# Second products of the first four chunks of a fused attention and softplus network: from one product of 512 columns to two of 256, all but the last of each block

## The chip, the cores and the metric

The kernel runs on one core of a Trainium2 chip. The metric is device time in microseconds (us) for one execution, and a kernel's time is the median of its runs. TensorE (PE in the profile) makes the matrix products; each product has a weight load of its own (PEld), which brings the stationary operand. VectorE (DVE) and ScalarE (ACT) do element work, and SyncE (SP) issues the transfers.

## The reference, cut to what matters

```
k_p, v_p = mean over 8 rows of k, v           # 576 rows become 72
attn     = softmax(q k_p^T / 8)               # 8 batches, 8 heads, head size 64
x        = attn v_p, as 4608 tokens x 512
h        = x @ w_in                           # 512 -> 2048      "first products"
g        = max(h, 0) + log1p(exp(-|h|))       # softplus
out      = g @ w_out                          # 2048 -> 512      "second products"
```

All is float32. A product of float32 accuracy is made of three products in a rounded float32 form (float32r): each operand is split into a high and a low part, and high x high, high x low and low x high are added in PSUM.

## The kernel before

The 4608 tokens are cut in 18 chunks of 256 (two tiles of 128 tokens). The 2048 hidden features are 16 groups of 128. For one chunk and one group, the first products make `h` (128 features x 256 tokens): four blocks of 128 input features, three products each, so 12 products with 256 moving columns (the tokens, `x`), the weights being stationary. ACT makes softplus of it twice, once rounded (`gh`) and once in full, and DVE subtracts to get the low part `gl`. The second products have 128 tokens of `gh` or `gl` as the stationary operand, and the weights `wo` (512 output columns) move. They add up in `acc`, one PSUM bank of 128 x 512 for each token tile.

There are three regimes:

- Chunks 0 to 2 (`feed`) run while the weights are still being loaded and split into high and low parts. First products are line 514, second products line 536 (`ffn2`): for each group 2 token tiles x 3 products, so 6 products of 512 columns, and 48 such blocks.
- Chunk 3 takes two groups at once (`pair1`, line 562, and `pair2`, line 603): 2 tiles x 2 groups x 3 = 12 products of 512 columns in each of 8 blocks.
- Chunks 4 to 17 save products with sums of quarters (`pair2_fast`, line 710). Here all products, first and second, have 256 columns. The second products take quarters of `wo` (its columns 0 to 255 or 256 to 511) or combined sums as the moving operand. The change doesn't touch them.

The order of the work is made while the program is built: a planner (`Order.run`) lists operations with estimated costs, in us, and places them engine by engine; each engine then runs its own list in that order and waits by semaphores. The second products are one operation each there, with written costs:

```
before2 = op(PE, 1.4, second, ...)          # feed: one ffn2 block
o = p2[c, u] = op(PE, 2.8, fn, wait, ...)   # chunk 3: one pair2 block
```

The `x` of chunks 0, 1, 3 and all later ones lies in two pairs of buffers of `xpool`; that of chunk 2 lies in the slots `Sa`, `Sb`, which later hold sums (`new_x`). In the built program's placement a partition's first byte of `wo`'s moving rows is at 64 modulo 128, in both halves of 256 columns, and all stationary `gh` and `gl` are at 0 modulo 128. For the first products the weights (stationary) are at 0 modulo 128, and `x` (moving) at 64 for all chunks but chunk 2, whose `x` is at 0.

Of the kernel before, what the change touches and what calls it, by code (L numbers as in the profile page):

```python
# [103 lines left out]
def pooled_attention_softplus_ffn(  # L104
# [9 lines left out]
    nc = tc.nc  # L114
    nc.scalar.preload_act_table_set("exp_and_others")
    B, H, S, D = q.shape
    NTOK, DM = out.shape
# [6 lines left out]
    T = 2  # L124
# [3 lines left out]
    FC = DFF // P  # L128
# [4 lines left out]
    FP = FC // 2  # L133
    O2 = DM // 2
# [367 lines left out]
    gs, accs = {}, {}  # L502
# [19 lines left out]
    def split_g(c, f, name):  # L522
# [2 lines left out]
        nc.vector.tensor_tensor(out=gl, in0=g, in1=gh.bitcast(F32), op=ALU.subtract)  # L525
        gs[c, f] = gh, gl

    def ffn2(c, f):
        if f == 0:
            accs[c] = [psum.tile([P, DM], F32, tag=b, name="acc") for b in acc_banks]  # L530
        gh, gl = gs.pop((c, f))
        hi, lo = wo[f]
        for t in range(T):
            ts = slice(t * P, (t + 1) * P)
            for j, (a, w) in enumerate(((gh, hi), (gh, lo), (gl, hi))):
                nc.tensor.matmul(out=accs[c][t], lhsT=a[:, ts], rhs=w,  # L536
                                 start=f == 0 and j == 0, stop=f == FC - 1 and j == 2)

    def copy_out(c, t, tag):
        o = one.tile([P, DM], F32, tag=tag, name="o")  # L540
# [53 lines left out]
    def pair2(c, u):  # L594

        if u == 0:
            accs[c] = [psum.tile([P, DM], F32, tag=b, name="acc") for b in acc_banks]
        g, gh, gl = gs.pop((c, u))
        for t in range(T):
            for k in range(2):  # L600
                hi, lo = wo[2 * u + k]
                for j, (a, w) in enumerate(((gh, hi), (gh, lo), (gl, hi))):
                    nc.tensor.matmul(out=accs[c][t], lhsT=a[:, 2 * k + t], rhs=w,  # L603
                                     start=u == 0 and k == 0 and j == 0,
                                     stop=u == FP - 1 and k == 1 and j == 2)

# [449 lines left out]
    def feed(c):  # L1058
        before1 = before2 = None
        acc_slots[c] = [Slot("bank") for _ in range(T)]  # L1060
        for f in range(FC):
            s, n, g, gh, gl = (Slot(x) for x in ("bank", "h", "g", "gh", "gl"))
            before1 = op(PE, 1.4, lambda f=f, s=s: ffn1_products(c, f, bank(s, "h")),
                         [before1, *x_done[c], *converted[f]], [s, n, *(acc_slots[c] if f == 0 else [])],
                         rest=8.4 * (FC - f) - LATER * c, first=LEAD * (N1 - 1 - c))
            a = op(ACT, act(CT), lambda f=f, s=s, gh=gh: softplus(c, f, s.tile, "gh" + gh.name), [before1, *exps],
                   [s, gh], table="softplus")
            d = op(ACT, act(CT), lambda f=f, s=s, g=g: softplus(
                c, f, s.tile, g.name), [a], [s, n, g], table="softplus")
            d = op(DVE, dve2(CT), lambda f=f, s=gl: split_g(c, f, s.name), [a, d], [g, gh, gl])  # L1070

            def second(f=f):
                if f == 0:
                    acc_banks[:] = [s.name for s in acc_slots[c]]
                ffn2(c, f)
            if (c, f) != (N1 - 1, FC - 1):
                before2 = op(PE, 1.4, second, [before2, d], [gh, gl, *acc_slots[c]],
                             rest=8.4 * (FC - f) - LATER * c + 6, first=200)
# [239 lines left out]
    def second_products(c, u, before):  # L1318
        fast = c >= NF
        wait, slots = p2[c, u]  # L1320
        wait = [before, *wait, *(t_ready.get(u, ()) if fast else ())]
        if u == 0:
            banks_of[c] = [Slot("acc") for _ in range(4 if fast else T)]
        banks = banks_of[c]

        def fn(which=(1, 2, 6, 7, 5, 3, 4)):
            if u == 0:
                (m_banks if fast else acc_banks)[:] = [s.name for s in banks if s.name]
            if fast:
                if u == 0 and which[0] == 5:  # L1330
                    m_banks[:] = m_banks[2:]
                pair2_fast(c, u, which)
            else:
                pair2(c, u)
        if not fast:
            o = p2[c, u] = op(PE, 2.8, fn, wait, [*slots, *banks])
            if u == FP - 1:
                output(c, [o], banks)
        elif u in (0, FP - 1):
            i, o = drained.get(c - 1, (None, None)) if u == 0 else (None, None)  # L1340
            i = op(PE, 12 * MM, lambda: fn((1, 2, 6, 7)), [*wait, i], [*slots, *banks[:2]])
            o = p2[c, u] = op(PE, 9 * MM, lambda: fn((5, 3, 4)), [i, o], [*slots, *banks[2:]])
            if u == FP - 1:
                output(c, [i, o], banks)
        else:
            o = p2[c, u] = op(PE, 21 * MM, fn, wait, [*slots, *banks])
        return o
# [25 lines left out]
    def last_of_first(before):  # L1373
        s = taken
        o = op(PE, 1.4, lambda: ffn2(N1 - 1, FC - 1), [before], s[:4])
        output(N1 - 1, [o], s[:T])
        return o
# [61 lines left out]
```

## Time and profile before

| | |
|---|---|
| median of 3 runs | 898.61 us (898.35 to 899.19) |
| the profiled execution's own time | 899.0 us |
| its span, first to last instruction | 897.3 us |
| granted TensorE clock | 0.998 |
| PE busy | 884.1 us, 99% of the span, 8308 products |
| DVE busy | 649.5 us, 72% |
| ACT busy | 407.7 us, 45% |
| line 536 (512 columns) | 288 products, 46.4 us to 190.5 us |
| line 603 (512 columns) | 96 products, 194.2 us to 243.5 us |

A busy PE says little, since products overlap and their ends are modelled: a product of 256 columns is given some 279 ns and the next starts long before. What a product costs is the distance from its start to the next one's start, and that is what the prediction reads from the timeline. In a timeline row, the first number is the start of a run of equal instructions and the second the time to the end of its last one.

### The profile page before, as it was taken

To read this page: it belongs to the slowest core of one execution; us is meant where nothing else is said; L and a number is where in the kernel's file an instruction comes from. 1 tells how busy PE (TensorE), PEld (TensorE's weight loads), DVE (VectorE), ACT (ScalarE), POOL (GpSimd) and SP (SyncE) were. 2 spreads that over 40 slices of the span, in tenths; PEclk is the share of its full clock that TensorE was granted. 3 is DMA by queue.
4 is the path that set the end of the run, shared out by engine and by line. 5 is a ranking of instruction groups with operands and counts; after the bars stand their busy time and mean duration, and the time that the engine had idled before them with its cause. 6 is when DMAs were issued, how large, how long until landed. Compare 5 with 4: busy or idle time off the path is not lost.

```text
span 897.3 us, 20507 instructions
## 1 busy us (share of the span) xinstructions
PE 884.1 (99%) x8308; PEld 836.7 (93%) x8308; DVE 649.5 (72%) x1601; ACT 407.7 (45%) x824; POOL 2.4 (0%) x19
## 2 busy tenths in 40 slices
PE   7999999999999999999999999999999999999997
PEld 3789989888999999999999999999999999999997
DVE  5899998888867768777667766777566565747454
ACT  4964343445353535444454435353545354434332
POOL 1000000000000000000000000000000000000000
PEclk9999999999999999999999999999999999999999
DMA  7975535545887678687658775787656565747472
GB/s 233 287 256 177 199 140 169 169 159 172 288 289 236 226 229 258 211 269 240 213 189 263 224 228 194 214 250 224 218 168 233 187 212 189 234 143 228 173 241 88
DMA packets 107085, 191.12 MB, mean 213 GB/s; under 512 B 46064, under 2 KB 60400, under 8 KB 106992
## 3 DMA queue, kind: packets, MB, share of 16 engines
q1 hardware_dynamic: 106992, 189.82, 65.0%
q8 instruction: 65, 1.06, 0.5%
q14 instruction: 28, 0.23, 0.1%
HBM read 167.25 MB, written 22.54 MB: 212 GB/s over the span
## 4 chain that ended last, share of the span: by engine, by line
PE 95%; DVE 2%; DMA 1%; SPq 1%; ACT 0%; issue 0%; DVEq 0%; ACTq 0%
PE h L562 37%; PE m L710 30%; PE acc L536 7%; PE h L514 7%; PE acc L603 3%; PE sc L379 2%; PE avp L481 2%; PE qTp L359 2%; PE ptp L440 2%; PE avp L488 1%; DMA wst<-in_moe_w_out_dram 1%; PE ltp L452 1%; DMA kvl<-in_v_dram 1%; ACT E L404 0%; SPq L331 0%; DVE o L731 0%
## 5 line engine op out<-in xcount | busy, mean ns | idle before, releaser
L562 PE MATMUL h<-x,w 128*128 128x256 f32 x2880 | 353.1, 279 | 0.0
L562 PEld LDWEIGHTS h<-x,w 128*128 128x128 f32 x2880 | 339.2, 188 | 1.0
L570 ACT ACTIVATE g<-h 128x512 f32<-128x512 f32 x120 | 71.8, 599 | 280.6 <-PE h L562 279.1
L710 PE MATMUL m<-w,so 128*128 128x256 f32 x1344 | 171.8, 277 | 0.0
L710 PEld LDWEIGHTS m<-w,so 128*128 128x128 f32 x1344 | 161.8, 188 | 0.1
L710 PE MATMUL m<-w,gh 128*128 128x256 f32 x672 | 130.7, 284 | 0.0
L621 DVE TENSOR_TENSOR sf<-g 128x128 f32<-128x128 f32 x112 | 32.7, 292 | 125.9 <-ACT g L570 125.3
L710 PEld LDWEIGHTS m<-w,gh 128*128 128x128 f32 x672 | 101.5, 188 | 1.7
L635 ACT CAST so<-sf 128x512 fp32r<-128x512 f32 x112 | 69.7, 622 | 58.1 <-DVE sf L624 57.0
L640 DVE TENSOR_TENSOR so<-sf,so 128x512 fp32r<-128x512 f32 x112 | 77.4, 691 | 23.2 <-ACT so L635 23.1
L710 PE MATMUL m<-w,gl 128*128 128x256 f32 x336 | 93.2, 277 | 0.0
L514 PEld LDWEIGHTS h<-x,w 128*128 128x128 f32 x576 | 71.0, 189 | 3.2 <-ACT g L519 0.4
L514 PE MATMUL h<-x,w 128*128 128x256 f32 x576 | 72.4, 279 | 0.0
L591 DVE TENSOR_TENSOR gl<-g,gh 128x384 fp32r<-128x384 f32 (+1 forms) x120 | 67.3, 561 | 0.4 <-ACT gh L584 0.2
L710 PEld LDWEIGHTS m<-w,gl 128*128 128x128 f32 x336 | 63.1, 188 | 0.0
L536 PE MATMUL acc<-w,g 128*128 128x512 f32 x192 | 60.9, 398 | 0.0
L584 ACT ACTIVATE gh<-h 128x384 fp32r<-128x384 f32 (+1 forms) x120 | 59.1, 492 | 0.0
L519 ACT ACTIVATE g<-h 128x256 fp32r<-128x256 f32 x96 | 32.0, 382 | 56.8 <-PE h L514 34.1
L731 DVE TENSOR_TENSOR o<-o,m 128x256 f32<-128x256 f32 x98 | 39.7, 418 | 3.3 <-ACT o L723 0.4
L536 PEld LDWEIGHTS acc<-w,g 128*128 128x128 f32 x192 | 33.6, 188 | 5.5
L536 PE MATMUL acc<-w,gl 128*128 128x512 f32 x96 | 38.0, 396 | 0.2 <-DVE gl L525 0.2
L386 DVE TENSOR_REDUCE mn<-sc 128x4 f32<-128x288 f32 x72 | 31.4, 451 | 8.3 <-PE sc L379 8.2
(170 smaller groups left out, 982.3 us busy)
## 6 DMA issues: line engine op xcount, KB each, us to landing
w<-wi SPq DMA_DIRECT2D x224, 512.0 KB
out_dram<-o SPq DMA_DIRECT2D x36, 256.0 KB
q<-in_q_dram SPq DMA_DIRECT2D x32, 256.0 KB
wst<-in_moe_w_in_dram SPq DMA_DIRECT2D x32, 256.0 KB
wst<-in_moe_w_out_dram SPq DMA_DIRECT2D x16, 512.0 KB
wi<-w SPq DMA_DIRECT2D x16, 512.0 KB
kst<-in_k_dram SPq DMA_DIRECT2D x24, 288.0 KB
vst<-in_v_dram SPq DMA_DIRECT2D x24, 256.0 KB
```

Of the source, the lines that this page charges most:

```text
L514: nc.tensor.matmul(out=ps[:, 0:CT], lhsT=row(w, kc), rhs=x[:, kc], start=first and kc == j == 0, stop=last and kc == KC - 1 and j == 2)
L519: nc.scalar.activation(out=g, in_=ps[:, 0:CT], func=AF.Softplus)
L536: nc.tensor.matmul(out=accs[c][t], lhsT=a[:, ts], rhs=w, start=f == 0 and j == 0, stop=f == FC - 1 and j == 2)
L562: nc.tensor.matmul(out=ps[:, k * CT:(k + 1) * CT], lhsT=row(w, kc), rhs=x_[c][i][:, kc], start=first and n == 0, stop=last and n == len(or ...
L570: nc.scalar.activation(out=g, in_=x.rearrange("p (b i) -> p b i", i=P), func=AF.Softplus)
L584: nc.scalar.activation(out=gh, in_=quarters(c, x.rearrange("p (b i) -> p b i", i=P)), func=AF.Softplus)
L591: nc.vector.tensor_tensor(out=gl, in0=quarters(c, g), in1=gh.bitcast(F32), op=ALU.subtract)
L621: tt(out=sf[:, 2], in0=g[:, 0], in1=g[:, 2], op=ALU.add)
L635: nc.scalar.copy(out=so[:, 0], in_=ss[c, u])
L640: nc.vector.tensor_tensor(out=so[:, 1], in0=sf, in1=so[:, 0].bitcast(F32), op=ALU.subtract)
L710: nc.tensor.matmul(out=ms[c][n], lhsT=x, rhs=y, start=u == 0 and j == 0 and n in (1, 6, 5, 4), stop=u == FP - 1 and j == 2 and n in (2, 7, ...
L731: nc.vector.tensor_tensor(out=o, in0=in0, in1=m[n], op=how)
```

## The change

A helper `add` makes the product of an `acc` tile either whole (512 columns) or as two halves of 256 columns with the same stationary operand, into the two halves of the bank. `whole` is true for the last of the products of each block alone (last tile, low part, and in `pair2` the second group). Of 48 x 6 + 8 x 12 = 384 products, 48 x 5 + 8 x 11 = 328 become two, and 56 stay whole: 712 in all. The sums that a bank collects are the same.

```
+    def add(acc, a, w, start, stop, whole):
+
+        n = DM if whole else O2
+        for i in range(0, DM, n):
+            nc.tensor.matmul(out=acc[:, i:i + n], lhsT=a, rhs=w[:, i:i + n],
+                             start=start and i == 0, stop=stop and i == DM - n)
+
     def ffn2(c, f):
...
-                nc.tensor.matmul(out=accs[c][t], lhsT=a[:, ts], rhs=w,
-                                 start=f == 0 and j == 0, stop=f == FC - 1 and j == 2)
+                add(accs[c][t], a[:, ts], w, f == 0 and j == 0, f == FC - 1 and j == 2,
+                    j == 2 and t == T - 1)
...
     def pair2(c, u):
...
-                    nc.tensor.matmul(out=accs[c][t], lhsT=a[:, 2 * k + t], rhs=w,
-                                     start=u == 0 and k == 0 and j == 0,
-                                     stop=u == FP - 1 and k == 1 and j == 2)
+                    add(accs[c][t], a[:, 2 * k + t], w, u == 0 and k == 0 and j == 0,
+                        u == FP - 1 and k == 1 and j == 2, k == 1 and j == 2 and t == T - 1)
```

The planner's costs and numbers are as before, so no operation moves: the lists of DVE, ACT, SP and POOL read alike, and so does PE's apart from the split. Of the PE list, this is the block of chunk 0, group 9 (`acc_694` and `acc_695` are the two token tiles, `w9` the weights), with the first products around it. Before:

```order
L514 MATMUL h_1587<-x_478,w10_1509 128x256
L536 MATMUL acc_694<-w9_1452,g_1579 128x512 x2
L536 MATMUL acc_694<-w9_1452,gl_1585 128x512
L536 MATMUL acc_695<-w9_1452,g_1579 128x512 x2
L536 MATMUL acc_695<-w9_1452,gl_1585 128x512
L514 MATMUL h_1618<-x_680,w9_1452 128x256 x2
```

And with the change (buffer numbers differ, since they count instructions):

```order
L514 MATMUL h_1712<-x_478,w10_1619 128x256
L532 MATMUL acc_694<-w9_1552,g_1704 128x256 x4
L532 MATMUL acc_694<-w9_1552,gl_1710 128x256 x2
L532 MATMUL acc_695<-w9_1552,g_1704 128x256 x4
L532 MATMUL acc_695<-w9_1552,gl_1710 128x512
L514 MATMUL h_1748<-x_680,w9_1552 128x256 x2
```

Six products of 512 columns have become ten of 256 and one of 512; its neighbours on PE are the same ones.

## The prediction

> **What bounds the kernel now.** I read the page's busy times and slices first, then the busy times by stage, then PE's timeline around the changed products. On the page:
>
> ```profile
> PE 884.1 (99%) x8308; PEld 836.7 (93%) x8308; DVE 649.5 (72%) x1601; ACT 407.7 (45%) x824; POOL 2.4 (0%) x19
> PE   7999999999999999999999999999999999999997
> DVE  5899998888867768777667766777566565747454
> ...
> PE 95%; DVE 2%; DMA 1%; SPq 1%; ACT 0%; issue 0%; DVEq 0%; ACTq 0%
> PE h L562 37%; PE m L710 30%; PE acc L536 7%; PE h L514 7%; PE acc L603 3%; PE sc L379 2%; PE avp L481 2%; PE qTp L359 2%; PE ptp L440 2%; PE avp L488 1%; DMA wst<-in_moe_w_out_dram 1%; PE ltp L452 1%; DMA kvl<-in_v_dram 1%; ACT E L404 0%; SPq L331 0%; DVE o L731 0%
> ...
> L536 PE MATMUL acc<-w,g 128*128 128x512 f32 x192 | 60.9, 398 | 0.0
> L536 PE MATMUL acc<-w,gl 128*128 128x512 f32 x96 | 38.0, 396 | 0.2 <-DVE gl L525 0.2
> ```
>
> PE is on 95% of the chain, and the two changed lines are 10% of it. Line 536 waited 0.2 us in all. But a busy PE is no proof, so the stages (columns: window, its length, then busy time and count of PE, PEld, DVE, ACT, POOL; clock; DMA share; GB/s):
>
> ```profile
> 64.00:100.00 36.00, 35.99 (x236) 32.08 (x235) 34.49 (x55) 14.35 (x36) 0.00 (x0) 1.00 0.58 190
> 152.00:190.00 38.00, 38.00 (x260) 33.79 (x259) 31.94 (x71) 14.74 (x37) 0.00 (x0) 1.00 0.43 139
> 190.00:245.00 55.00, 55.00 (x500) 49.01 (x499) 46.66 (x99) 26.67 (x48) 0.00 (x0) 1.00 0.69 229
> ```
>
> From 64 to 245 us, where nearly all of the change lies, PE has no gap: what a product costs more or less shows in the end, unless another engine becomes late. The nearest is DVE, with 34.49 of 36.00 us in the first of these stages. The clock is full, so no price here changes with the throttle.
>
> **The price of a whole product and of a half.** Differences of starts are prices. One stretch of PE's timeline in chunks 0 to 2, and one in the steady part, where all products have 256 columns:
>
> ```profile
> 113.37 0.62 PE L536 MATMUL acc<-w,g 128*128 128x512 f32 x2
> ...
> 116.16 1.53 PE L514 MATMUL h<-x,w 128*128 128x256 f32 x12
> 117.53 0.62 PE L536 MATMUL acc<-w,g 128*128 128x512 f32 x2
> ```
>
> ```profile
> 432.20 2.88 PE L562 MATMUL h<-x,w 128*128 128x256 f32 x24
> 434.92 0.39 PE L710 MATMUL m<-w,gh 128*128 128x256 f32 x2
> 435.14 0.28 PE L710 MATMUL m<-w,gl 128*128 128x256 f32 x1
> 435.26 0.39 PE L710 MATMUL m<-w,gh 128*128 128x256 f32 x2
> 435.49 0.28 PE L710 MATMUL m<-w,gl 128*128 128x256 f32 x1
> 435.60 1.52 PE L710 MATMUL m<-w,so 128*128 128x256 f32 x12
> ```
>
> In the steady part 24 products of 256 columns take 434.92 - 432.20 = 2.72 us, 113.3 ns each. The six after them, to 435.60, take 0.68 us, again 113.3 each. These six are the nearest rows to what the change makes: `gh` and `gl` stationary, and the first and then the second half of `wo` moving, at the same place modulo 128 bytes as in the changed blocks.
>
> In the early stretch, 12 whole products and the 12 of 256 columns behind them take 117.53 - 113.37 = 4.16 us. With 113.3 for each of the 12, the whole ones cost (4.16 - 1.36) / 12 = 233.3 ns. (By 116.16 - 113.37 alone they cost 232.5, and the 12 behind them 114.2 in place of 113.3: the first of those still pays for the change of width, so I count the two together.) Two halves cost 226.7, so a pair saves 6.7 ns.
>
> The Trainium skill speaks against this: "TensorE: Matmul & The Clock Gate", section on the back-to-back issue gap, gives a product N columns / 2.4 GHz plus a fixed 2.5 ns when warm. By that a whole product is 215.8 ns and two halves 218.3, 2.5 ns more for each pair, some 0.8 us slower in all. The trace differs on both widths, 233.3 and 113.3: here the part above the columns' own time is not a fixed one for each product.
>
> The upper end of a half's price is in rows too. These are pieces of the chain of waits in order of time (start, length, what):
>
> ```profile
> 60.19 2.87 PE h L514 x24
> ...
> 420.21 2.73 PE h L562 x24
> ...
> 426.27 2.83 PE h L562 x24
> ...
> 437.46 2.72 PE h L562 x24
> ```
>
> The first, 2.87 / 24 = 119.6 ns, is the first use of chunk 2's `x`, the one that lies at 0 modulo 128 as its weights do. The changed products don't have that placement, so I don't take it. The piece at 426.27, 2.83 / 24 = 117.9 ns, has the good placement and still the slower spacing, all along the run; it comes soon after scores (line 379) on PE. The pieces at 420.21 and 437.46 are at 113.8 and 113.3, and so is the run from 432.20 above. So a run of halves behind other PE work may stay in the slow spacing: one run of these four. At 117.9 a pair costs 235.8, 2.5 ns more than a whole product. The bounds for a pair are thus -6.7 and +2.5 ns, and +5.9 by the chunk-2 row.
>
> **The sum.** 328 pairs. PE still waits for others before 64.5 us:
>
> ```profile
> 64.07 0.40 PE L536 MATMUL acc<-w,gl 128*128 128x512 f32 x1
> 64.48 0.39 PE L514 MATMUL h<-x,w 128*128 128x256 f32 x1
> ```
>
> The last product before 64.48 is 0.41 us from the next start in place of 0.23: PE waited. What the four blocks before it gain (20 pairs, 0.13 us) is lost there. 308 pairs are left: 308 x 6.67 = 2.05 us.
>
> Ten of the remaining 52 blocks start directly behind transposes, scores or attention products, four of `ffn2` and six of `pair2`; one of them:
>
> ```profile
> 193.45 1.03 PE L359 MATMUL qTp<-ident,q 128*128 128x128 f32 x8
> 194.24 0.71 PE L603 MATMUL acc<-w,gh 128*128 128x512 f32 x2
> ```
>
> They hold 4 x 5 + 6 x 11 = 86 pairs. At 235.8 in place of 226.7 they would take back 86 x 9.2 = 0.79 us; with one in four, as above, 0.2 us. The sum is -2.05 + 0.2 = -1.85 us.
>
> What is added and costed at nothing: 328 more weight loads, since PEld x8308 equals PE x8308 on the page, so each product has its own; the steady rows have one for each 256 columns too, within the 113.3. The instructions are 656 more of 20507, and their fetching is 0.5% of the DMA engines' span. No DMA, no buffer and no step of another engine is added or moved. The wait for `gl` stands on the fifth product in place of the third, 0.45 us behind the block's start in place of 0.46.
>
> Where PE comes earlier, what is late next? DVE, which splits the weights into high and low parts (line 849 is the last step of a group) just ahead of their first use. The tightest case is group 14:
>
> ```profile
> 149.55 4.33 PE L514 MATMUL h<-x,w 128*128 128x256 f32 x36
> 153.71 0.62 PE L536 MATMUL acc<-w,g 128*128 128x512 f32 x2
> ```
>
> ```profile
> 146.32 0.43 DVE L525 TENSOR_TENSOR gl<-g 128x256 fp32r<-128x256 f32 x1 [0.69 <-ACT g L519]
> ...
> 151.21 0.69 DVE L849 TENSOR_TENSOR w<-wg,w 128x512 fp32r<-128x512 f32 x1
> ```
>
> The 36 products are groups 13, 10 and 14 of 12 each, so group 14 starts at 149.55 + 24/36 x 4.16 = 152.32, and its weights are ready at 151.90: 0.42 us of slack. Up to there 31 of the counted blocks have saved 31 x 5 x 6.67 ns = 1.03 us. If DVE came no earlier, 0.6 us would be lost. But DVE itself stood 0.69 us at 146.32, waiting for ACT's `g`, which waits for PE's `h`; that wait shrinks as PE comes earlier, so DVE moves along. I take nothing for it and keep 0.6 us as the bound.
>
> The profiled execution took 899.0 us, 0.4 above the median 898.61. From 899.0 the sum gives 897.15; from the median 896.8, which is the forecast: -0.21%. A measurement of this kernel can tell about 0.2% (1.8 us) from no change, so the forecast stands right on that line.
>
> **The rivals.**
>
> 1. DVE takes part of the gain back. For it: 34.49 of 36.00 us busy, 0.42 us of slack; against: the 0.69 us wait that gives way. Gain 1.85 - 0.6 = 1.25: 897.4 us. Chance 0.15, within 0.2%.
> 2. Halves cost more here than in the steady part, since each product of these blocks has a cost of its own, or since two products that load the same stationary tile one after the other are spaced worse. At 116.7 ns a half nothing changes, 898.6 us; at the 117.9 of the row from 426.27 it is 308 x 2.5 ns more, 899.4 us. Against it are the six products from 434.92, though none of them loads the same tile twice. Chance 0.10, within 0.2%. The rule of the Trainium skill's page above ("TensorE: Matmul & The Clock Gate", back-to-back issue gap) is of this kind, and by its figures too the time is 899.4; the two widths that the trace shows speak against it.
> 3. Slower: the lone whole product at the end of a block. In all rows above, whole products come in runs, and the products of 256 columns behind them find back to 113.3. If a single one throws the run behind it into the spacing of 117.9 or 119.6, then the 384 first products of chunks 0 and 1 and the 192 of chunk 3 cost 4.6 to 6.3 ns more: 576 x 4.6 to 6.3 = 2.6 to 3.6 us, against the 1.85 saved: 899.4 to 900.4. It decides from half of these products on (1.85 / 3.6), and passes 0.2% with all of them at 119.6. Nothing in the trace shows a lone one. Chance 0.08, 0.05 of it slower by over 0.2%.
> 4. More than forecast: no block falls into the slow spacing (2.05 us), and some first products behind the blocks that are slow now become fast, 0.11 us for each run of 24 (2.83 against 2.72 in the rows above); with four of them, an estimate, 2.5 us in all: 896.1 us. Chance 0.10, faster.
>
> **How the numbers follow.** The forecast's own case, halves at 113.3 nearly everywhere and PE still the bound, has chance 0.57 and lies between 896.3 (no slow block, 896.56, less 0.26 as the fastest run shown is below its median) and 897.4 (all 86 pairs slow). The line at 0.2% is 896.8, near its middle; I put 0.34 below it and 0.23 above. With rival 4 that makes 0.44 for faster. Within 0.2%: 0.23 + 0.15 + 0.10 + 0.03 = 0.51. Slower: 0.05. The range over all is 895.9 to 898.8: below it lies a part of rival 4, above it rival 3 and the upper half of rival 2, some 0.15 in all. The forecast's own range is 896.3 to 897.4.
>
> **What would show each step.** In the changed kernel's timeline, ten halves of a block (line 532) from start to start should take 1.13 us, and a block of `pair2`, with 22 halves and one whole, 2.73 in place of 2.80. The first products behind them should keep 2.72 to 2.73 for 24 in chunks 0 and 1. Starts in the steady part should come 1.8 us earlier than now, with the same spacing. Rival 1 would show as a wait of line 514 on DVE's line 849 near 150 us; rival 3 as 2.8 us and more for 24 first products of chunk 0, 1 or 3. The forecast is wrong if halves cost over 116.7 ns, or if the runs behind a lone whole product change.

## The result: slower by 0.33%

| | before | after |
|---|---|---|
| median, us | 898.77 (895.95 to 900.1, 9 runs) | 901.65 (899.58 to 904.56, 9 runs) |
| ratio | | 1.0033 [1.002, 1.0046] |
| profiled execution: own time, span | 899.0, 897.3 | 904.56, 902.8 |
| products on PE | 8308 | 8636 |

The profiled execution of the changed kernel was the slowest of its nine, so its span shows more than the medians differ by. Five more runs gave 901.51 against 898.2, ratio 1.0035 [1.0021, 1.0049] (the last experiments below). A ratio has its own working and leaves disturbed runs out, so it isn't always the quotient of the two medians beside it. The page after the change:

```profile
PE 886.7 (98%) x8636; PEld 855.2 (95%) x8636; DVE 650.0 (72%) x1601; ACT 407.7 (45%) x824; POOL 2.4 (0%) x19
PE   6899999999999999999999999999999999999997
...
PE 92%; DMA 3%; DVE 2%; SPq 2%; ACT 1%; issue 0%; DVEq 0%; ACTq 0%
...
L532 PE MATMUL acc<-w,g 128*128 128x256 f32 x384 | 61.1, 281 | 0.0
...
L532 PE MATMUL acc<-w,gl 128*128 128x256 f32 (+1 forms) x200 | 50.6, 312 | 0.2 <-DVE gl L525 0.2
```

Both changed lines are now line 532 (first products keep line 514 in chunks 0 to 2, and are line 569 from chunk 3 on; `m` is line 716). PE has 328 products and weight loads more, all of DVE's and ACT's counts are as before, and line 532 waited 0.2 us as line 536 had. PE's part of the chain is 92% in place of 95%, since this chain passes through two transfers in the steady part (`w<-wi`, 9.17 us up to 504.0 us, and `vst<-in_v_dram`, 7.72 us up to 616.6) and through SP's queue for 6.6 us more at the start; at 41 us this execution is just 0.20 us later than before's. The two transfers come up again with theory C in the experiments. The busy times by stage (columns as in the prediction) say that nothing else became the bound:

```profile
64.00:100.00 36.00, 35.94 (x293) 34.93 (x292) 34.27 (x54) 14.18 (x34) 0.00 (x0) 1.00 0.58 188
152.00:190.00 38.00, 38.00 (x323) 36.79 (x323) 32.12 (x72) 15.33 (x39) 0.00 (x0) 1.00 0.42 142
190.00:245.00 55.00, 55.00 (x589) 53.21 (x588) 46.65 (x99) 26.87 (x48) 0.00 (x0) 1.00 0.67 222
```

PE is busy but for 0.06 us, at full clock, and still later. So the time is in what a product costs. PE's timeline of chunks 0 to 2 (start, time to the end of the last one, what):

```profile
107.08 0.64 PE L532 MATMUL acc<-w,g 128*128 128x256 f32 x4
107.55 0.39 PE L532 MATMUL acc<-w,gl 128*128 128x256 f32 x2
107.77 0.62 PE L532 MATMUL acc<-w,g 128*128 128x256 f32 x4
108.23 0.39 PE L532 MATMUL acc<-w,gl 128*128 128x512 f32 x1
108.45 1.58 PE L514 MATMUL h<-x,w 128*128 128x256 f32 x12
109.87 0.63 PE L532 MATMUL acc<-w,g 128*128 128x256 f32 x4
110.34 0.40 PE L532 MATMUL acc<-w,gl 128*128 128x256 f32 x2
110.57 0.63 PE L532 MATMUL acc<-w,g 128*128 128x256 f32 x4
111.04 0.40 PE L532 MATMUL acc<-w,gl 128*128 128x512 f32 x1
111.28 2.99 PE L514 MATMUL h<-x,w 128*128 128x256 f32 x24
```

The first block, from 107.08, starts with the spacing of the chunk-2 run ahead of it, falls to 113 ns by its fifth half, and ends with a whole product that costs 226 ns (108.23 to 108.45). Behind that one, all is slow: the 12 first products take 1.42 us, 118 ns each; the ten halves from 109.87 to 111.04 take 1.17 us, 117 to 118 each; the lone whole product 0.24; and the 24 first products behind it 2.83 us, up to 114.11, 117.9 each. Before, the same 24 started at 110.64 and took 2.73, up to the row at 113.37 that the prediction shows. The slow spacing then lasts through every block up to the next run of chunk 2, at 136.7 us.

The second place is one that the change doesn't touch: the first stretch of chunk 4, from the last block of chunk 3 to the next transposes. The chain of waits in order of time (start, length, what), before and then after:

```profile
249.00 2.72 PE h L562 x24
251.72 2.38 PE m L710 x21
...
264.30 0.87 PE ptp L440 x8
```

```profile
250.53 2.83 PE h L569 x24
253.36 2.47 PE m L716 x21
...
266.43 0.87 PE ptp L440 x8
```

The runs of 24 take 2.83 in place of 2.72 and the runs of 21 take 2.47 in place of 2.38. The eight transposes at the end of the stretch start 266.43 - 264.30 = 2.13 us later; 0.20 of these were there at 41 us, before any changed product, and 1.93 arose in between. The same distance, taken at other places:

| us later than before, from 41 us on | 100 | 146 | 186 | 204 | 246 | 268 | 550 | 650 | end |
|---|---|---|---|---|---|---|---|---|---|
| after | 0.38 | 1.03 | 1.07 | 0.99 | 1.22 | 1.93 | 2.67 | 4.48 | 5.37 |
| after, profiled again | 0.36 | 1.01 | 1.05 | 0.97 | 1.20 | 1.91 | 2.27 | 2.76 | 2.76 |
| before, profiled again | -0.60 | -0.60 | -0.59 | -0.58 | -0.58 | -0.58 | -0.56 | -0.74 | 0.14 |

Up to 268 us the two profiles of the changed kernel agree within 0.03 us. Behind that they don't agree with each other: 2.6 of the first one's 5.37 us are missing in the second.

### The profile page after: what moved, and what is told of

It reads as the page before. It is cut to its first block, busy times and chain, and to the rows that moved or that the text cites. A ratio compares the mean times of both kernels' runs of the same rounds, so it can differ in the third digit from the quotient of the medians.

```text
span 902.8 us, 21165 instructions
## 1 busy us (share of the span) xinstructions
PE 886.7 (98%) x8636; PEld 855.2 (95%) x8636; DVE 650.0 (72%) x1601; ACT 407.7 (45%) x824; POOL 2.4 (0%) x19
## 4 chain that ended last, share of the span: by engine, by line
PE 92%; DMA 3%; DVE 2%; SPq 2%; ACT 1%; issue 0%; DVEq 0%; ACTq 0%
PE h L569 36%; PE m L716 29%; PE acc L532 10%; PE h L514 7%; PE sc L379 2%; PE avp L481 2%; PE ptp L440 1%; PE qTp L359 1%; PE avp L488 1%; DMA w<-wi 1%; DMA vst<-in_v_dram 1%; PE ltp L452 1%; DMA wst<-in_moe_w_out_dram 1%; DMA kvl<-in_v_dram 1%; SPq L900 1%; ACT E L404 0%
## 5 line engine op out<-in xcount | busy, mean ns | idle before, releaser
L532 PE MATMUL acc<-w,g 128*128 128x256 f32 x384 | 61.1, 281 | 0.0
L532 PEld LDWEIGHTS acc<-w,g 128*128 128x128 f32 x384 | 52.7, 189 | 0.6
L532 PE MATMUL acc<-w,gl 128*128 128x256 f32 (+1 forms) x200 | 50.6, 312 | 0.2 <-DVE gl L525 0.2
```

The costliest lines, as they stand in the source:

```text
L532: nc.tensor.matmul(out=acc[:, i:i + n], lhsT=a, rhs=w[:, i:i + n], start=start and i == 0, stop=stop and i == DM - n)
```

## The experiments

A table behind the last experiment puts all variants side by side. The expectations speak of these theories: **A**, a lone whole product in a stream of halves throws the spacing from 113.3 to 117.9 ns; **B**, the rival, two halves that load the same stationary tile one after the other are spaced slowly by themselves; **C**, waits later in the kernel make the difference; **D**, the steady part loses in any variant.

**No whole product at all** (1), against B:

```
-                    j == 2 and t == T - 1)
+                    False)
```

and the same in `pair2`.

> No product stays whole: all 384 become two halves. Theory A (a lone whole product leaves the 256-column products behind it in the spacing of 117.9 ns): with no whole product the runs of chunks 0, 1 and 3 are at 113.3 ns, the first chunk-4 products start 1.8 to 2.4 us earlier than in the kernel before (now 1.4 later), and the time is 896.3 to 897.2 us. Theory B (two halves that load the same stationary tile cause the slow spacing, the whole one has no part in it): 117.9 ns in the runs as in the changed kernel, chunk 4 starts 1.4 us late or more, 901 to 902 us. Theory C (the early spacing explains little, the rest is later waits that came with another timing): about 900 to 901 us, whatever the spacing.

898.92 against 898.03, ratio 0.9997 [0.9981, 1.0013]. The timeline at the same place:

```profile
109.39 2.88 PE L514 MATMUL h<-x,w 128*128 128x256 f32 x24
112.11 0.62 PE L532 MATMUL acc<-w,g 128*128 128x256 f32 x4
...
113.47 0.62 PE L532 MATMUL acc<-w,g 128*128 128x256 f32 x4
```

Twelve halves take 113.47 - 112.11 = 1.36 us, 113.3 each, and 24 first products 2.72. The halves and their stationary tiles are those of the changed kernel, but for the last pair of each block: B falls. In chunk 4 this kernel too takes 2.83 us for 24 first products, and loses 0.8 us there, about as much as the changed kernel and without any whole product: its spacing had turned slow in chunk 3 behind scores (line 379). So a lone whole product isn't the only thing that turns the spacing.

**The last two whole** (2), **the last three whole** (3), **the first one whole** (4): the number and the place of the whole products. In `ffn2` (and likewise in `pair2`):

```
-                    j == 2 and t == T - 1)
+                    j >= 1 and t == T - 1)         # 2
+                    t == T - 1)                    # 3
+                    j == 0 and t == 0)             # 4
```

> The last two products of each block stay whole, 272 are split. Theory A: two whole products in a row let the runs behind come back to 113.3 ns as the runs of 2, 4, 6 and 12 do in the kernel before; chunk 4 starts some 1.6 us earlier than in the kernel before, 897.0 to 897.5 us. Theory B: slow spacing as in the changed kernel, 901 us. Theory C: 900 to 901 us.

> The last three products of each block stay whole, 216 are split. Theory A in its first form (only a lone one does it): runs at 113.3 ns, chunk 4 starts 1.3 us earlier than before, 897.3 to 897.8 us. Theory A in its second form (an odd number of whole products in a row does it, since whole products alternate between 231 and 236 ns): runs at 117.9 ns, chunk 4 starts 1.3 to 1.8 us late, 900.5 to 902 us. Theory B: 900 to 901 us.

> The first product of each block stays whole in place of the last; as many are split as in the changed kernel (328). Theory A: it is as lone there, so the halves behind it and the first products after the block are at 117.9 ns, chunk 4 starts 1.4 us late or more, 901 to 902 us. Theory B: the same, 901 to 902 us. A rival to both (it is the edge between a whole product and the next block's waits that does it, not its being alone): 113.3 ns behind it and 896.7 to 897.2 us.

With two, 898.94, ratio 1.0008 [0.9994, 1.0022]; with three, 899.63, 1.0014 [0.9998, 1.0031]; with the first one alone 901.56, 1.003 [1.0013, 1.0048], the loss of the changed kernel again, so it isn't the end of the block that does it. Two whole (the second `gh` product, in the row with x3, and `gl`):

```profile
113.95 0.62 PE L532 MATMUL acc<-w,g 128*128 128x256 f32 x4
114.41 0.39 PE L532 MATMUL acc<-w,gl 128*128 128x256 f32 x2
114.64 0.61 PE L532 MATMUL acc<-w,g 128*128 128x256 f32 x3
115.09 0.40 PE L532 MATMUL acc<-w,gl 128*128 128x512 f32 x1
115.33 1.53 PE L514 MATMUL h<-x,w 128*128 128x256 f32 x12
116.69 0.62 PE L532 MATMUL acc<-w,g 128*128 128x256 f32 x4
```

12 first products take 1.36 us: they come back to 113.3. Three whole:

```profile
111.25 0.62 PE L532 MATMUL acc<-w,g 128*128 128x256 f32 x4
111.71 0.39 PE L532 MATMUL acc<-w,gl 128*128 128x256 f32 x2
111.93 0.62 PE L532 MATMUL acc<-w,g 128*128 128x512 f32 x2
112.40 0.39 PE L532 MATMUL acc<-w,gl 128*128 128x512 f32 x1
112.63 0.63 PE L532 MATMUL acc<-w,g 128*128 128x256 f32 x4
113.10 0.40 PE L532 MATMUL acc<-w,gl 128*128 128x256 f32 x2
113.33 0.62 PE L532 MATMUL acc<-w,g 128*128 128x512 f32 x2
113.79 0.40 PE L532 MATMUL acc<-w,gl 128*128 128x512 f32 x1
114.03 1.53 PE L514 MATMUL h<-x,w 128*128 128x256 f32 x12
115.39 0.62 PE L532 MATMUL acc<-w,g 128*128 128x256 f32 x4
```

Six halves take 111.93 - 111.25 = 0.68 us (113); behind three whole products the next six take 113.33 - 112.63 = 0.70 (117); behind three more, the 12 first products take 115.39 - 114.03 = 1.36 (113). So it alternates. And with the first one whole, 12 first products in the slow spacing:

```profile
115.45 1.58 PE L514 MATMUL h<-x,w 128*128 128x256 f32 x12
116.86 0.64 PE L532 MATMUL acc<-w,g 128*128 128x512 f32 x3
```

These are all places from 64.5 to 250 us where whole products stand between products of 256 columns, at least three ahead and nine behind. The state ahead is the median spacing of the three, that behind the median of the nine; fast is under 115 ns, slow 115 to 119. Places with a first product of chunk 2 among these twelve are left out, since its runs have 120 of their own:

| whole products in a row | fast ahead: stays, turns slow | slow ahead: stays, turns fast |
|---|---|---|
| 1, last (after; again) | 1, 13; 0, 13 | 21, 3; 21, 4 |
| 1, first (4) | 0, 8 | 20, 4 |
| 2 (2) | 22, 1 | 1, 1 |
| 3 (3) | 1, 8 | 2, 13 |
| 6 and 12 (before) | 14, 0 | none |

A single whole product turns the fast spacing slow in 34 of 35 places, and leaves the slow one as it is in 62 of 73. Two keep it fast in 22 of 23, six and twelve in 14 of 14. Three turn fast to slow in 8 of 9 places and slow to fast in 13 of 15. A holds, with "an odd number" in place of "a lone one" as far as one and three were tried; why the odd ones turn it, and why three turn the slow spacing back and one doesn't, isn't shown.

The times bear A out less well than the spacings do. Of (1) to (8) only (4) and (6) came out in the range that A gave; (1), (2), (5) and (8) were above theirs, by 0.8 us for (5) up to 3.7 us and more for (8), (3) fell between the ranges of A's two forms, and (7) was 1.9 us above the range for a cause in the placement. A rests on the timelines.

**Halves in chunks 0 to 2 alone** (5) and **in chunk 3 alone** (6, with the lone whole product as in the change). The edits are `False` in `ffn2` with `True` in `pair2`, and `True` in `ffn2` with `pair2` as changed:

> All products of chunks 0 to 2 are halves, those of chunk 3 are whole again as in the kernel before (288 split). Theory A (the spacing of 113.3 or 117.9 ns is a state that lasts from product to product until something flips it; a lone whole product flips the fast one, the runs of 12 whole ones of chunk 3 end in the fast one): the stretch to 185 us gains 1.4 to 1.9 us against the kernel before as in the run with all halves, chunk 4 starts in the fast state (its first products from 246 to 265 us at 113.3 ns, where the run with all halves had 117.9), time 896.3 to 897.3 us. Theory D (the steady part loses 1.2 to 1.7 us in whatever variant, by its own doing): 897.6 to 898.6 us.

> Only chunk 3 as in the changed kernel (88 split, its eight last products whole), chunks 0 to 2 whole as before. Theory A: up to 190 us as before; in chunk 3 the first products behind the lone whole ones at 117.9 ns, about even there (0 to 0.5 us), and the slow state carried into chunk 4's first stretch, 0.65 us there: 898.7 to 899.6 us. A rival (the loss of the changed kernel is made in chunks 0 to 2 alone): 897.8 to 898.3 us. Theory D: over 899.6 us.

898.14 against 898.25, ratio 0.9994 [0.9978, 1.001]; and 898.78, 1.0002 [0.9992, 1.0012]. The first stretch of chunk 4 in the chain of each:

```profile
254.76 2.72 PE h L569 x24
257.48 2.38 PE m L716 x21
```

```profile
258.02 2.83 PE h L569 x24
260.85 2.47 PE m L716 x21
```

Twelve whole products per block in chunk 3 hand a fast spacing on to chunk 4 (2.72); halves with a lone whole one hand on a slow one (2.83), and that costs (6) 0.71 us from 246 to 268 us, with chunk 3 itself at +0.15. The 0.7 us of the changed kernel in chunk 4 thus come from chunk 3's blocks. (1) shows that the lone product isn't needed for that: what chunk 3 had before, and hands on fast, are its whole products in runs.

**The operand of chunk 2 moved** by 64 bytes, in the kernel before (7), and with halves in chunks 0 to 2 besides (8). Its `x` lies at 0 modulo 128 and its first run takes 119.6 ns. Of before, the edit (besides this, `so`, in the same slot `Sb`, lies 64 bytes further, and all buffers lie 512 bytes lower):

```
-            x_[c] = [one.tile([P, HP, CT], F32R, tag=tag, name="x") for tag in ("Sa", "Sb")]
+            x_[c] = [one.tile([P, HP * CT + 16], F32R, tag=tag, name="x")[:, i:i + HP * CT].rearrange(
+                "p (m i) -> p m i", m=HP) for tag, i in (("Sa", 16), ("Sb", 0))]
```

> The kernel before with the x of chunk 2 placed 64 bytes on modulo 128 (all other operands keep their place modulo 128; everything lies 512 bytes lower). Does the place of the operands make the 119.6 ns of chunk 2's first products? If so these 192 products are at 113.3 ns, 1.2 us less, 896.6 to 897.2 us. If their 119.6 has another cause (the engines' load at those times, the weights' groups): no change, 898 us.

> Chunks 0 to 2 all halves, chunk 3 whole, and the x of chunk 2 moved as well. Theory A with the place: 1.4 to 1.9 and 1.2 us less, 895.0 to 895.8 us. But chunk 2's runs, which threw the state into the fast one on leaving them, no longer do so: if a slow state once entered then lasts through chunks 0 to 2, up to 2 us come back and it is 897 us. Theory D: 896.2 to 897.2 us.

899.11 against 898.25, 0.9997 [0.9985, 1.0008]; and 900.72, 1.0025 [1.0012, 1.0038]. Of (7), the chain and then the timeline:

```profile
58.64 2.72 PE h L515 x24
```

```profile
114.75 1.58 PE L515 MATMUL h<-x,w 128*128 128x256 f32 x12
116.16 0.62 PE L537 MATMUL acc<-w,g 128*128 128x512 f32 x2
```

The first run of chunk 2 takes 2.72 us in place of 2.87, as it should. But later runs in the whole early part stand at 118 ns (12 in 1.41 us): from 64.5 to 190 us, 8 first products are left at 120 to 126 ns, where 114 were, and those at 117 to 119 have gone from 99 to 361. The chunk-2 runs had a use: what follows one of them falls back to 113, as the block from 107.08 above shows. With it gone, (8) stays slow in 444 of its 508 first products there that are at one spacing or the other, with no whole product near; what turned them slow there isn't shown.

**Both kernels once more** (9, 10), unchanged, for what differs from one execution to the next.

> The changed kernel once more. What is open: at 268 us its first profile was 1.9 us behind the kernel before, and another 3.5 us came later, where the code is the same. If those are events of that one execution (a wait at 503 and at 620 us, the stretches from 618 and 642 us in the slow spacing): they stand elsewhere or are missing now, the first 268 us again 1.6 to 2.1 us behind, and the time is 900 to 901.7 us. If they belong to the changed kernel: the same stretches slow and the same waits again, 901.5 us or more.

> The kernel before once more, for the same question: chunks 0 to 4 as in its first profile, spacing block by block (a state that is set by the order of the work), and the stretch from 666 to 690 us, which was fast in its first profile and slow in five of the others, either fast again (the state there hangs on the kernel) or slow (it changes from one execution to the next). 896 to 900 us.

901.51 against 898.2, ratio 1.0035 [1.0021, 1.0049], and a profiled execution of before of 898.46. They give the second and third row of the table of distances above. First after and then before, in the chain of waits, late in the steady part:

```profile
677.02 2.72 PE h L569 x24
679.74 2.38 PE m L716 x21
```

```profile
678.28 2.83 PE h L562 x24
681.11 2.47 PE m L710 x21
```

Here it is the kernel before that has the wider spacing, from 666 to 690 us, 0.9 us in all; in its first profile 24 products there took 2.72. D falls with that as a cause: from 268 us to the end the second profile of before loses 0.72 us against the first one, and the variants lose 0.3 to 2.8. (5)'s median lay in D's range, though.

C rested on the first profile after the change, with these waits of PE up to 504 and 621.7 us (in all, times, longest):

```profile
PE sc L379 <- DVE E L393: 1.0, 1, 1.0
...
PE h L569 <- DMA w<-wi: 0.4, 1, 0.4
```

PE has neither wait in the second profile, which has the same 1.9 us up to 268. But C isn't done with: the second profile loses 0.46 us at the first of these places and 0.49 at the second, together its whole way from 1.8 to 2.76. At the first, its weight loads wait for the same transfer:

```profile
503.43 1.90 PEld L569 LDWEIGHTS h<-x,w 128*128 128x128 f32 x16 [0.18 <-DMA w<-wi]
```

Both profiles of before pass there without a loss, and so do (1), (2), (3), (6) and (7), while (4), (5) and (8) lose 0.9 to 1.2 us at the first place, and (8) 0.6 at the second. (5) had come there earlier than before, and (4) and (8) later. Why the transfer lands late in some profiles stays open.

All variants side by side. "Early" is the distance from before in the one profile, from 41 to 268 us; "median" is the ratio's excess over one with its interval, times 898 us. Up to 64.5 us PE still waits for others, and executions of one kernel differ there: before's second profile gains 0.57 us, (6) 0.84. From 64.5 us on, before's second profile stands at -0.01, (6) at +0.86, and the others within 0.07 of the table:

| | early, us | median, us |
|---|---|---|
| after; again | +1.93; +1.91 | +3.0 [1.8, 4.1]; +3.1 [1.9, 4.4] |
| 1 all halves | -0.74 | -0.3 [-1.7, 1.2] |
| 2 last two whole | -1.01 | +0.7 [-0.5, 2.0] |
| 3 last three whole | -0.01 | +1.3 [-0.2, 2.8] |
| 4 first one whole | +2.39 | +2.7 [1.2, 4.3] |
| 5 halves in chunks 0 to 2 | -1.52 | -0.5 [-2.0, 0.9] |
| 6 change in chunk 3 alone | +0.02 | +0.2 [-0.7, 1.1] |
| 7 chunk 2's `x` moved | +0.40 | -0.3 [-1.3, 0.7] |
| 8 as 7, with halves in chunks 0 to 2 | +0.92 | +2.2 [1.1, 3.4] |

The early part lies inside the interval in eight of ten. It is below the middle in most, by up to 1.7 us. So the changed kernel's early part explains 1.9 of its 3 us; of the remaining 1 us or so, the second profile has 0.85, at the two places of C's waits, and its cause stays open. No variant is shown to be faster than before: (5) gains most early, and its median can't be told from no change.

## Why the prediction was wrong, step by step

The forecast was 896.8, with 0.05 for slower; measured 901.65, above the range's end of 898.8. Rival 3 happened.

- **What bounds the kernel**: right. PE is busy without a gap from 64 to 245 us, and what a product costs more showed one for one.
- **The price of a half, 113.3 ns, with one run in four slow among 86 pairs**: this step failed. The six rows from 434.92 come from a stretch without any whole product, and don't show what a half costs in a stream with them. From 64.5 to 190 us, 111 halves stood at about 113 and 284 at 117 to 119. Expected were ten halves in 1.13 us; they took 1.17 from 109.87.
- **"The products of 256 columns behind them find back to 113.3"**, said of whole products in runs and taken over for the lone one: this is the other half of the failed step. 310 first products stood at 117 to 119 ns where 99 had; of the 30 runs of 12 of chunks 0 and 1 there, 22 were slow where 3 had been.
- **The sum.** For 64.5 to 190 us, 395 counted halves are 198 pairs, which at the predicted prices save 198 x 6.7 = 1.3 us. 284 slow halves x 4.6 ns give back 1.3, and 211 more slow first products x 4.6 ns cost 1.0. That makes +1.0; the distance grew by 1.06. The distances of starts, added up in both traces from 64.5 to 186 us, give the same: the changed blocks took 0.05 us more, the first products of chunks 0 and 1 0.93 more, those of chunk 2 0.09 more. The steady part was to start 1.8 us earlier, and starts 1.93 later at 268 us. The saving did exist: without whole products there, (1) and (5) had gained 1.5 us by 186 us.
- **Rival 3** had the mechanism, and a size of 2.6 to 3.6 us for the first products against a saving of 1.85. It happened with other terms: fewer first products turned (those directly behind a run of chunk 2 stayed fast, and chunk 3 cost only 0.15 us), the halves turned too and lost the saving, and chunk 4 began in the slow spacing, 0.7 us in a stretch that the prediction didn't look at. Its chance, 0.08, was argued from "nothing in the trace shows a lone one", which was a reason to call it unknown. The rows held a warning: the prediction quoted a run at 117.9 ns with a good placement, "all along the run", with no cause for it but scores on PE nearby. A spacing that lasts through 24 equal products is something carried over, and the change touches what carries it.
- **Rival 1**: line 514 never waited for DVE's weights near 150 us, and DVE's 34.27 of 36.00 us stayed without effect.
- **Rival 2**, dearer halves: the two halves with one stationary tile don't cost more by themselves, (1). The Trainium skill's rule that it named ("TensorE: Matmul & The Clock Gate", back-to-back issue gap: 2.5 ns on each product, which that section gives for an isolated one) gives the right sign but not the cause: by it (1), with the most products, would be the slowest, and its ratio is 0.9997 where the changed kernel's is 1.0033.
- **Costed at nothing**: 328 weight loads, right, as (1) has 56 more of them, and 445 of its 528 halves between 64.5 and 190 us stand at 113 ns.

## What to carry to other kernels

The price of a product on a full PE can depend on the products before it, so a price has to be read from rows with the same neighbours; where none exist, a change that makes a new neighbourhood (here a lone wide product in a stream of narrow ones) deserves an unknown term: the difference of the spacing's two values, times all products behind it. Whoever halves such products does all of a stretch, or leaves two or a long run whole, and looks at the first stretch behind the edit too; none of these is shown to be faster here than no change. A run that looks dearer than it should, like chunk 2's, may be what sets its neighbours back: moving it gained nothing.

## What the runs showed of the hardware that was not expected

The distance of products of 256 columns took two values, 113.3 and 117.9 ns, at the same operands' placement and full clock. The value persisted through whole runs and blocks: in the changed kernel the 219 products of 256 columns from 108.45 to 136.6 us stood at 117 to 119, 117.8 on average. An odd number of products of 512 columns (one or three) turned 113.3 into 117.9 in 42 of 44 places, two left it in 22 of 23; a lone whole product itself took 226 ns behind halves at 113 and mostly 235 or 236 behind halves at 118. Runs with `x` at 0 modulo 128, 119.6 to 120 ns each, were mostly followed by 113 where other products of 256 columns or six whole ones came next; a lone whole product directly behind such a run, in (4), was followed by 118 in all seven places.
